# Talking-heads attention and two expert layers on one core: three steps instead of two regrouped inside SBUF, before the rows are stored

## The chip, the cores and the metric

The kernel runs on one core of a Trainium2 chip. The metric is the device time of one execution in microseconds (us). Before the change the median of three runs is 1144.06 us (1140.52 to 1148.41).

## The reference

Four batches of attention with 12 heads, 448 positions and 64 numbers per head; scores are mixed across the heads before the softmax and again behind it. The result goes through two blocks of dense layers. All is float32; the dense matmuls are made of three products of rounded halves.

```python
scores = scale * np.matmul(q, k.transpose(0, 1, 3, 2))
scores = np.einsum('bhij,hg->bgij', scores, w_pre)
attn = softmax(scores)
attn = np.einsum('bhij,hg->bgij', attn, w_post)
x = rows of np.matmul(attn, v)            # 1792 x 768
x = ((x @ w1) * (x @ w2) @ w3) @ w_out
x = np.maximum(np.maximum(x @ m1, x @ m2), x @ m3) @ m_out
```

## The kernel before

**Scores.** A *unit* makes the scores of two heads for 128 queries (a row block): eight matmuls `s<-kall,q` (line 344; the first six units use the three PSUM pairs m, p and s in turn), one eviction with the scale (lines 359 on ACT, 361 on DVE), and a store to DRAM (`sdram`). The six units of batch 0's first row block are evicted into six slices of the large tile `a` (a part of the plan named `arow`); all others go through a ring of two buffers `s`, so the third of them can be evicted only when the store of the first has been read out.

**Regrouping.** The softmax needs the 12 heads of a query beside each other on the partitions. A *step* takes 20 queries: `regroup` brings them into one of three buffers `x`, normally from `sdram` by two copies `x<-sdram`, which wait for the stores of the whole row block. The first steps of batch 0 (those below `FIRST` queries) are copied from `a` inside SBUF, by four copies `x<-a` of five partitions into sixty.

**Step.** The mix `m<-x,kp` (line 407), the maximum `nmax` on DVE (line 411), two exponentials `e` on ACT (line 414), the weights of the second mix (lines 419 to 421), and the second mix `p<-kwr,e` (line 445), whose copy into `a` must wait until the rows in `a` have been copied and stored.

**Dense work beside it.** From the start the kernel also multiplies w3 and w_out together (line 605). Both arrive as 64-bit floats by loads on the POOL queue, 16 tiles of w_out (`early`) and 16 halves of w3 (`wraw`, a ring of three); DVE and ACT turn each into a pair of halves (lines 523 to 528, 535, 537, 570, 571: `hhi`, `hlo` for the first eight tiles of w_out, `yhi`, `ylo` for the others). A load into a used buffer waits until DVE has converted what was in it. Later come the dense layers (line 685) and, behind the planned part, the last two batches (line 221).

**Order.** `Plan` lists every operation with its key (when it is wanted), its inputs and an assumed duration; `order()` runs through them once and writes a fixed order for each engine and for the DMA queue of SP. Engines are in order: an instruction that waits holds all behind it. A DMA that follows eight others on its queues waits until the oldest of these has landed.

Of the kernel before, what the change touches and what calls it, by code (L numbers as in the profile page):

```python
# [18 lines left out]
P = 128  # L19
GI = 10  # L20
# [10 lines left out]
AHEAD = 2  # L31
# [3 lines left out]
HP = H // 2  # L35
# [8 lines left out]
def blocks_of(p):  # L44

    i = 2 * GI * p
    return [[max(0, min(GB, S - i - GI * c - GB * u)) for u in range(2)] for c in range(2)]
# [10 lines left out]
SWITCH = 0.21  # L58
LAND = 2.0
RATE = 0.29  # L60
FIRST = 2 * 2 * GI
BACK = 2.5
STAY = 0.5
QUEUED = 8
# [113 lines left out]
def attention_talking_heads_moe_kernel(  # L178
# [26 lines left out]
    sdram = [dram.tile([S, H, S], F32, name=f"sdram_{b}") for b in range(B)]  # L205
# [59 lines left out]
    def turn(ring, n):  # L265
        used[ring] = used.get(ring, -1) + 1
        return used[ring] % n

    def dma(eng, key, out, src, nbytes, reads=(), writes=()):
        plan(  # L270
            eng, 0.55 if eng == "POOL" else 0.42, key,
            lambda e: ENG[e].dma_start(out() if callable(out) else out, src() if callable(src) else src),
            reads, writes, bytes=nbytes,
        )
# [45 lines left out]
    def load_k(b, pairs, key, eng="SP"):  # L320
        a, z = pairs[0], pairs[-1] + 1
        dma(eng, key, kall[:, a:z], kT[b, :, a:z], 229e3 * (z - a), (), [("k", x) for x in pairs])

    def load_q(b, r, key, eng="SP", after=()):
        w = min(P, S - P * r)
        slot = turn("q", 2)
        dma(eng, key, qs[slot].rearrange("p x j -> p (x j)")[:, :HP * w], qT[b, :, HP * P * r:HP * (P * r + w)],
            3072 * w, list(after), [("q", slot)])
        return slot

    def unit(b, r, u, slot, key, room="s"):

        whole = P * (r + 1) <= S
        parts = [(u, 0), (u, HB)] if whole else [(2 * u, 0), (2 * u + 1, 0)]
        pt = {"m": pm, "p": pp, "s": pz}[room]

        w = min(P, S - P * r)
        q = qs[slot].rearrange("p x j -> p (x j)")[:, :HP * w].rearrange("p (x j) -> p x j", x=HP)

        def multiply(_):  # L340
            for c, (pr, i) in enumerate(parts):
                for o in range(2):
                    sl = slice(o * D, (o + 1) * D)
                    nc.tensor.matmul(  # L344
                        pt[HB * c:HB * c + HB, o, :S], q[sl, pr, i:i + HB], kall[sl, pr], start=True, stop=True
                    )

        bank_of = [(room, x) for x in range(2)]
        plan("PE", 0.76, key, multiply, [("k", pr) for pr, _ in parts] + [("q", slot)], bank_of, mode="q")
        if r == 0 and b == 0:  # L350
            out, where = at.rearrange("p t h i -> p (t h i)")[:, 2 * S * u:2 * S * (u + 1)], ("arow", u)
            out = out.rearrange("p (o j) -> p o j", o=2)
        else:
            n = turn("s", 2)
            out, where = st[n], ("st", n)

        def evict(e):
            if e == "ACT":
                nc.scalar.activation(out, pt[:, :, :S], AF.Copy, scale=D ** -0.5)
            else:  # L360
                nc.vector.tensor_scalar_mul(out, pt[:, :, :S], D ** -0.5)  # L361

        plan({"ACT": 0.95, "DVE": 1.12}, 0, key + 0.05, evict, bank_of, [where])
        if whole:
            x = 0 if r or b else FIRST
            dma("SP", key + 0.06, sdram[b][P * r + x:P * r + P, 2 * u:2 * u + 2], out[x:], 3584 * (P - x), [where],
                [("sd", b, r, u)])
        else:
            for c, (pr, _) in enumerate(parts):
                dma("SP", key + 0.06, sdram[b][P * r:S, 2 * pr:2 * pr + 2], out[HB * c:HB * c + HB], 229e3,  # L370
                    [where], [("sd", b, r, pr)])

    def regroup(b, p, key):
        n = turn("x", AHEAD + 1)
        x = xr[n]
        i = 2 * GI * p
        rows = range(i // P, (min(i + 2 * GI, S) - 1) // P + 1)
        reads = [("sd", b, r, pr) for r in rows for pr in range(HP)]
        if b == 0 and i < FIRST:
            row = at.rearrange("p t h i -> p (t h i)")[:, :H * S]  # L380
            for c in range(2):
                for u in range(2):
                    z = i + GI * c + GB * u
                    dma("SP", key, x[HB * u:HB * u + MR, c], row[z:z + GB], 108e3,
                        [("arow", pr) for pr in range(HP)], [("x", n, u, c)])
        elif i + 2 * GI <= S:
            src = sdram[b][i:i + 2 * GI].rearrange("(c u i) h j -> u (i h) c j", c=2, u=2)
            for u in range(2):
                dma("SP", key, x[HB * u:HB * u + MR], src[u], 215e3, reads, [("x", n, u, 0), ("x", n, u, 1)])
        else:  # L390
            for u, m in enumerate(blocks_of(p)[0]):
                src = sdram[b][i + GB * u:i + GB * u + m].rearrange("i h j -> (i h) j")
                dma("SP", key, x[HB * u:HB * u + m * H, 0], src, 21504 * m, reads, [("x", n, u, 0), ("x", n, u, 1)])
        return n
# [67 lines left out]
    def load_v(b, key, after=()):  # L462
        n = S // P
        dma("SP", key, vt[:, :n], v[b, :P * n].rearrange("(c p) e -> p c e", p=P), 1180e3, (), [("v", 0)] + [("v", 0, x, z) for x in range(n) for z in range(2)])
        dma("SP", key, vt[:S - P * n, n], v[b, P * n:], 197e3, list(after), [("v", 1)])
# [564 lines left out]
    LAST = len(steps)  # L1030
# [14 lines left out]
    def attention_parts():  # L1045

        load_k(0, [0, 1], -20.0, "ACT")
        slot = load_q(0, 0, -20.0)
        load_k(0, [2, 3], -19.9)
        load_k(0, [4, 5], -19.8, "ACT")  # L1050
        block_diagonals(-19.0)
        for u in range(HP):
            unit(0, 0, u, slot, -8.0 + 0.1 * u, "mps"[u % 3])
        todo = [(0, r, u, (0.5 * u, 3 + u, 8.5 + 0.5 * u)[r - 1])
                for r in range(1, 4) for u in range(HP if r < 3 else 3)]
        for b in range(1, B):
            todo += [(b, r, u, NP * b - 11 + 6 * r + u) for r in range(4) for u in range(HP if r < 3 else 3)]
        due = {}
        for b, r, u, s in todo:
            due.setdefault(int(s), []).append((b, r, u))  # L1060
        slots = {}
        xn = {}
        for s in range(AHEAD):
            xn[s] = regroup(*steps[s], -7.0 + 0.1 * s)
        slots[0, 1] = load_q(0, 1, -5.6, after=[("arow", 2)])
        yield -1.0
        en = {}
        for s in range(LAST + LAG):
            if s == 1:
                load_v(0, 3.0, [("arow", 5)])  # L1070
            for d in (s + 2,):
                for b, r, u in due.get(d, []):
                    if u == 0 and (b, r) not in slots:
                        slots[b, r] = load_q(b, r, s)
                    if u == 0 and r == 0 and b:
                        for x in range(0, HP, 2):
                            load_k(b, [x, x + 1], s + 0.1 * x)
            if s + AHEAD < LAST:
                xn[s + AHEAD] = regroup(*steps[s + AHEAD], s - 0.5)
            for x, (b, r, u) in enumerate(due.get(s, [])):  # L1080
                unit(b, r, u, slots[b, r], s + 0.5 * x)
            if s < LAST:
                en[s] = softmax(*steps[s], xn[s], s)
            if s >= LAG:
                b, p = steps[s - LAG]
                post(b, p, en[s - LAG], s)
                if p == NP - 1 or p % CP == CP - 1:
                    attend(b, p, s + 0.97)
                    if p == NP - 1 and b + 1 < B:
                        load_v(b + 1, s + 1.0)  # L1090
            yield s + 0.03
# [16 lines left out]
    def summing():  # L1108
        yield TURN + 0.9
        yield from sum_parts(sums_at)  # L1110

    streams = [attention_parts(), dense_stream(), summing(), second_stream(), tail_stream()]
    heads = [(-20.0 + x, x) for x in range(5)]
    heapq.heapify(heads)
    pool_users = []
    while heads:
        _, x = heapq.heappop(heads)
        n = len(plan.ops)
        key = next(streams[x], None)
# [62 lines left out]
```

## Time and profile before

| | |
|---|---|
| median of three runs | 1144.06 us |
| the profiled execution | 1145.06 us |
| its span, first to last instruction | 1143.3 us |
| outside the span | 1.8 us |
| TensorE (PE) busy | 1102.1 us, 96% of the span |
| DVE, ACT busy | 782.7, 566.2 us |
| mean granted clock | 0.984 of full speed |

Busy time of PE is 96%, but in the first of forty slices it is 3 tenths. Idle time of another engine matters only where PE waits for it. The granted clock is the share of 2.4 GHz that TensorE was given; 0.50 is 1.2 GHz.

### The profile page before, as it was taken

Reading aid. Unit: us, or ns where it says so; the run is one execution under the profiler, and the core shown is the slowest. Engines: PE = TensorE matmul, PEld = TensorE weight load, DVE = VectorE, ACT = ScalarE, POOL = GpSimd, SP = SyncE. Lnnn points to the kernel's source line nnn. Section 1 sums busy time; section 2 is a strip of 40 time slices with the busy share of each in tenths; the row PEclk is TensorE's granted clock in tenths of the full one; section 3 lists DMA queues with packets and bytes.
Section 4 is the critical chain, followed back from the end, with each engine's and each line's share of the span. In section 5 each row is a group of like instructions: output and inputs, shape, how many; then the busy total and the mean of one; then the engine's idle time right before and its main releaser. Section 6 shows DMA issues by size and latency. Waiting matters only on the chain.

```text
span 1143.3 us, 29211 instructions
## 1 busy us (share of the span) xinstructions
PE 1102.1 (96%) x12348; PEld 889.4 (78%) x12348; DVE 782.7 (68%) x1343; ACT 566.2 (50%) x1071; POOL 73.6 (6%) x141
## 2 busy tenths in 40 slices
PE   3999999999999999999999989998999999999998
PEld 1466777787877877777777868887988899888877
DVE  3666785686766777767576676774877764587874
ACT  4576475566654677655445353533433343333331
POOL 3100010000000000000110101100000000000000
PEclk8799999999999999999999999999999999999999
DMA  8798887989874999888899898856433421233343
GB/s 305 217 334 247 282 292 256 311 297 319 303 260 155 311 332 303 291 268 283 284 312 316 271 308 267 283 195 222 148 117 97 120 77 46 76 99 116 107 115 117
DMA packets 106205, 258.95 MB, mean 226 GB/s; under 512 B 20278, under 2 KB 57162, under 8 KB 106074
## 3 DMA queue, kind: packets, MB, share of 16 engines
q1 hardware_dynamic: 88474, 175.79, 47.7%
q0 software_dynamic: 15584, 77.62, 20.5%
q10 hardware_dynamic: 2016, 3.67, 0.9%
q8 instruction: 97, 1.59, 0.6%
q14 instruction: 34, 0.28, 0.1%
HBM read 174.27 MB, written 81.91 MB: 224 GB/s over the span
## 4 chain that ended last, share of the span: by engine, by line
PE 84%; DMA 6%; issue 4%; DVE 3%; ACT 2%; POOL 0%; SPq 0%; DVEq 0%; ACTq 0%; POOLq 0%
PE w L685 28%; PE w L221 8%; PE p L445 7%; PE p L479 6%; PE p L221 6%; PE m L407 6%; PE w L605 6%; PE m L221 6%; PE s L221 5%; PE s L344 5%; DMA x<-a 1%; DMA sdram<-a 1%; DMA wc<-kept_b 1%; DMA vlo<-sums_o 1%; DMA wc<-kept_m 1%
## 5 line engine op out<-in xcount | busy, mean ns | idle before, releaser
L445 PEld LDWEIGHTS p<-kwr,e 60*64 60x64 f32 x5760 | 103.3, 137 | 45.3 <-issue 28.4
L411 DVE TENSOR_REDUCE nmax<-m 128x2 f32<-128x896 f32 (+1 forms) x92 | 100.1, 1088 | 53.7 <-PE m L407 53.2
L414 ACT ACTIVATE e<-m,nmax 128x448 f32<-128x448 f32 (+1 forms) x184 | 115.0, 633 | 36.6 <-DVE nmax L411 36.1
L407 PE MATMUL m<-x,kp 60*64 60x448 f32 x720 | 98.0, 565 | 16.7 <-DMA x<-a 13.0
L445 PE MATMUL p<-kwr,e 60*64 60x60 f32 x5760 | 106.4, 221 | 5.0 <-DVE xlo L489 2.9
L277 ACT COPY a<-p 128x480 f32<-128x480 f32 (+1 forms) x97 | 53.5, 574 | 93.5 <-PE p L445 84.9
L685 PE MATMUL w<-yhi,whi 128*128 128x448 f32 x216 | 83.3, 385 | 0.0
L685 PE MATMUL w<-yhi,wlo 128*128 128x448 f32 x216 | 79.4, 368 | 0.0
L685 PE MATMUL w<-ylo,whi 128*128 128x448 f32 x216 | 79.3, 367 | 0.0
L344 PE MATMUL s<-kall,q 64*64 64x448 f32 x640 | 79.0, 564 | 0.2 <-DVE s L361 0.2
L479 PEld LDWEIGHTS p<-a,v 128*64 128x64 f32 x1536 | 73.7, 137 | 5.9 <-issue 4.8
L479 PE MATMUL p<-a,v 128*64 128x120 f32 (+1 forms) x1536 | 77.6, 260 | 0.0
L685 PE MATMUL w<-xhi,whi 128*128 128x448 f32 x192 | 73.8, 384 | 0.0
L277 DVE COPY a<-p 128x480 f32<-128x480 f32 (+1 forms) x83 | 53.2, 652 | 29.9 <-ACT a L277 23.1
L685 PE MATMUL w<-xhi,wlo 128*128 128x448 f32 x192 | 70.2, 366 | 0.0
L685 PE MATMUL w<-xlo,whi 128*128 128x448 f32 x192 | 70.0, 365 | 0.0
L747 ACT CAST whi<-wlo 128x768 fp32r<-128x768 f32 x39 | 32.6, 835 | 73.6 <-DMA wlo<-sums_m 17.9
L685 PE MATMUL w<-hhi,whi 128*128 128x448 f32 x168 | 64.1, 382 | 2.6 <-ACT whi L660 1.8
L661 DVE TENSOR_TENSOR wlo<-wlo,whi 128x768 fp32r<-128x768 f32 (+1 forms) x52 | 52.8, 1015 | 20.1 <-ACT whi L660 19.8
L407 PEld LDWEIGHTS m<-x,kp 60*64 60x64 f32 x720 | 24.0, 135 | 53.7 <-issue 37.3
L685 PE MATMUL w<-hhi,wlo 128*128 128x448 f32 x168 | 61.5, 366 | 0.8 <-DVE wlo L661 0.8
L221 PE MATMUL p<-t,vhi 128*128 128x448 f32 x204 | 61.7, 372 | 0.5 <-DVE r L934 0.4
(237 smaller groups left out, 2531.3 us busy)
## 6 DMA issues: line engine op xcount, KB each, us to landing
x<-sdram SPq DMA_DIRECT2D x172, 210.0 KB
sdram<-s SPq DMA_DIRECT2D x66, 448.0 KB
wraw<-in_wm POOLq DMA_DIRECT2D x18, 768.0 KB, 7.1
wlo<-kept_m SPq DMA_DIRECT2D x27, 384.0 KB
wlo<-kept_w SPq DMA_DIRECT2D x18, 512.0 KB
wraw<-in_w3T POOLq DMA_DIRECT2D x16, 512.0 KB, 7.2
kept_m<-wc SPq DMA_DIRECT2D x18, 384.0 KB
wc<-kept_m POOLq DMA_DIRECT2D x18, 384.0 KB, 6.0
```

The source lines that it names most:

```text
L221: nc.tensor.matmul(out, w, r, start=(k == 0), stop=(k == 3 * n_k - 1))
L277: (nc.scalar.copy if e == "ACT" else ENG[e].tensor_copy)(out, src)
L344: nc.tensor.matmul(pt[HB * c:HB * c + HB, o, :S], q[sl, pr, i:i + HB], kall[sl, pr], start=True, stop=True)
L407: nc.tensor.matmul(pm[HB * c:HB * c + HB, u, :S], kp[sl], x[sl, c], start=True, stop=True)
L411: plan("DVE", 1.1, key + 0.01, lambda _: nc.vector.tensor_reduce(out=nmax[:r], in_=pm[:r, :, :S], axis=AX.X, op=ALU.max, negate=True), m_b ...
L414: plan("ACT", 0.85, key + 0.02, lambda _, u=u: nc.scalar.activation(e_[:r, u], pm[:r, u, :S], AF.Exp, bias=nmax[:r, u:u + 1], scale=1.0, a ...
L445: nc.tensor.matmul(pt[HB * side:HB * side + HB, c, t, :, u * GB:u * GB + m], e_[sl, u, j:j + HB], kwr[sl, u, :, :m], start=True, stop=True,)
L479: nc.tensor.matmul(pt[o * D:(o + 1) * D, x, pr % 3, :], vt[:, jc, h * D:(h + 1) * D], a[:, jc, h, :], start=(jc == 0), stop=(jc == JC - 1),)
L605: nc.tensor.matmul(pw[b][:, :FW], w, r, start=(k == 0 and i == 0), stop=(k == KH - 1 and i == 2))
L661: plan("DVE", 0.16 + 0.8 * f, key - 0.9, lambda _: nc.vector.tensor_sub(lo, t, hi.bitcast(F32)), h, l)
L685: nc.tensor.matmul(pw[w][:, :S], u, r, start=(k == 0 and i == 0), stop=(k == nk - 1 and i == 2))
L747: nc.scalar.copy(hi, t)
```

## The change

`FIRST` goes from 40 to 60 queries, so that step 2 too is copied from `a`, and the first row block is stored from row 60 on: 68 rows in place of 88. The six stores of these rows are collected in `later` and listed behind the first three regroupings, with a later key (1.5 in place of 0.06 behind the unit's), and each now waits for all six evictions. Step 2 is regrouped at the start; in the loop the next one is step 3.

```diff
-FIRST = 2 * 2 * GI
+FIRST = 3 * 2 * GI
...
+    later = []
+
     def unit(b, r, u, slot, key, room="s"):
...
             x = 0 if r or b else FIRST
-            dma("SP", key + 0.06, sdram[b][P * r + x:P * r + P, 2 * u:2 * u + 2], out[x:], 3584 * (P - x), [where],
-                [("sd", b, r, u)])
+            reads = [where] if r or b else [("arow", y) for y in range(HP)]
+            later.append(lambda: dma(
+                "SP", key + (0.06 if r or b else 1.5), sdram[b][P * r + x:P * r + P, 2 * u:2 * u + 2], out[x:], 3584 * (P - x), reads,
+                [("sd", b, r, u)]))
+            if r or b:
+                later.pop()()
...
-        for s in range(AHEAD):
+        for s in range(AHEAD + 1):
             xn[s] = regroup(*steps[s], -7.0 + 0.1 * s)
+        while later:
+            later.pop(0)()
...
-            if s + AHEAD < LAST:
+            if AHEAD < s + AHEAD < LAST:
                 xn[s + AHEAD] = regroup(*steps[s + AHEAD], s - 0.5)
```

The changed program's lines stand 2 to 8 further down; the operations are named the same. Its orders differ as follows.

SP's queue from its start, before (`q` are queries, `kall` keys, `sdram_75` the score rows of batch 0 in DRAM):

```order
L272 DMA q<-in_qT 128x768
L272 DMA kall<-in_kT 128x896
L272 DMA sdram_75<-a 88x896 x6
L272 DMA x<-a 60x1x448 x8
L272 DMA q<-in_qT 128x768
L272 DMA x<-sdram_75 60x2x448 x2
L272 DMA sdram_75<-s 128x896
L272 DMA x<-sdram_75 60x2x448 x2
```

and of the changed kernel:

```order
L272 DMA q<-in_qT 128x768
L272 DMA kall<-in_kT 128x896
L272 DMA q<-in_qT 128x768
L272 DMA x<-a 60x1x448 x12
L272 DMA sdram_75<-a 68x896 x6
L272 DMA sdram_75<-s 128x896
L272 DMA x<-sdram_75 60x2x448 x2
L272 DMA sdram_75<-s 128x896
L272 DMA q<-in_qT 128x768
L272 DMA sdram_75<-s 128x896
```

The copies inside SBUF stand ahead of the stores now, the second row block's queries are loaded at once, and its first store and the copies of step 3 stand behind the six stores.

PE's start, behind its first five units, of the changed kernel (before, the sixth unit is followed by the first mix at once):

```order
L346 MATMUL s<-kall,q 64x448 x16
L611 MATMUL w<-hhi,whi 128x384
L611 MATMUL w<-hlo,whi 128x384
L611 MATMUL w<-hhi,wlo 128x384
L611 MATMUL w<-hhi,whi 128x384
L611 MATMUL w<-hlo,whi 128x384
L611 MATMUL w<-hhi,wlo 128x384
L413 MATMUL m<-x,kp 64x448 x4
```

Three units of the second row block and the dense work of two tiles of w_out have come ahead of the first mix.

ACT, where the third unit of the second row block is evicted (`s<-s`), and what stands behind it up to the twelfth tile of w_out (the last `yhi`), in the changed kernel:

```order
L576 CAST yhi<-v 128x384 x2
L420 ACTIVATE e,den<-m,nmax 128x448
L277 COPY t<-w 128x384
L361 ACTIVATE s<-s 128x896
L533 ACTIVATE wraw<-wraw 128x512
L531 ACTIVATE wc<-wc 128x512
L533 ACTIVATE early<-early 128x384
L541 CAST whi<-wc 128x512
L531 ACTIVATE v<-v 128x384
L576 CAST yhi<-v 128x384
```

and before:

```order
L570 CAST yhi<-v 128x384
L277 COPY t<-w 128x384
L359 ACTIVATE s<-s 128x896
L570 CAST yhi<-v 128x384
L527 ACTIVATE early<-early 128x384
```

Before, it is the fourth unit of the second row block that is evicted at this place; in the changed kernel it is the third.

## Rows read from the trace of the kernel before

**Rows 1.** Page, 40 slices: busy tenths of PE.
```profile
PE   3999999999999999999999989998999999999998
```
**Rows 2.** Windows: us, PE, PEld, DVE, ACT, POOL busy (instructions), granted clock, DMA share, GB/s.
```profile
0.00:65.00 65.00, 41.35 (x232) 19.80 (x236) 35.99 (x77) 36.66 (x76) 16.58 (x34) 0.77 0.82 273
```
**Rows 3.** Waits, 0 to 60 us: total us, times, longest.
```profile
POOL early L272 <- DVE v L523: 23.3, 4, 10.9
PE m L407 <- DMA x<-a: 13.0, 2, 12.6
ACT e L414 <- DVE nmax L411: 10.2, 1, 10.2
ACT s L359 <- PE s L344: 4.4, 1, 4.4
```
**Rows 4.** Timeline of SP's queue: start, us, what.
```profile
8.24 6.06 SPq L272 DMA_DIRECT2D sdram<-a  x6
14.35 13.63 SPq L272 DMA_DIRECT2D x<-a  x8
```
**Rows 5.** Timeline of PE and ACT: start, us, what, wait ahead of it.
```profile
25.33 1.72 PE L407 MATMUL m<-x,kp 60*64 60x448 f32 x2 [12.58 <-DMA x<-a]
27.51 5.01 PE L407 MATMUL m<-x,kp 60*64 60x448 f32 x6 [0.46 <-DMA x<-a]
62.08 0.90 ACT L359 ACTIVATE s<-s 128x896 f32<-128x896 f32 x1
64.44 1.37 PE L344 MATMUL s<-kall,q 64*64 64x448 f32 x8
```
**Rows 6.** Windows: first the columns of rows 2, then PE alone with its clock, DMA share, GB/s.
```profile
20.00:22.00 2.00, 0.00 (x0) 0.00 (x0) 1.69 (x4) 1.73 (x4) 0.54 (x1) 0.50 0.71 286
...
0.00:14.30 14.30, 7.29 (x48) 1.00 0.88 307
33.50:36.00 2.50, 1.72 (x8) 0.50 0.32 125
```
**Rows 7.** DMA queues, 33.5 to 36 us: packets, MB, share of 16 engines.
```profile
q1 hardware_dynamic: 103, 0.17, 18.0%
q0 software_dynamic: 41, 0.14, 14.2%
```
**Rows 8.** DMA issues, 0 to 60 us: operation, times, KB each (us to landing).
```profile
early<-in_w_out POOLq DMA_DIRECT2D x16, 384.0 KB, 8.5
wraw<-in_w3T POOLq DMA_DIRECT2D x7, 512.0 KB, 7.9
sdram<-a SPq DMA_DIRECT2D x6, 308.0 KB
sdram<-s SPq DMA_DIRECT2D x3, 448.0 KB
...
q<-in_qT SPq DMA_DIRECT2D x3, 384.0 KB
kall<-in_kT ACTq DMA_DIRECT2D x2, 448.0 KB
x<-a SPq DMA_DIRECT2D x8, 105.0 KB
```
**Rows 9.** Timeline of POOL: start, us, what, wait ahead of it.
```profile
50.33 0.53 POOL L272 DMA_DIRECT2D wraw<-in_w3T  x1 [12.81 <-DVE v L523]
50.85 2.66 POOL L272 DMA_DIRECT2D early<-in_w_out  x5
```
**Rows 10.** Chain of waits, 300 to 400 us: start, us, what.
```profile
308.69 0.75 PE m L407 x8
...
311.12 5.06 PE w L685 x24
...
339.79 1.42 PE w L685 x6
341.20 0.91 PE s L344 x8
```

## Prediction

> **What bounds the kernel now.** I read the page's slices first: PE is busy 3 tenths of the first 28.6 us and nearly all of every later slice [rows 1]. The window of the first 65 us has PE busy for 41.35 of them [rows 2]. So a microsecond saved before 65 us should arrive at the end of the kernel, as long as PE's later work stays the same.
>
> The waits name what is late at the start [rows 3]. PE waits 13.0 us for the copies `x<-a`, and behind the first mix everything stands in line: ACT waits 10.2 us for the maximum, DVE sits in front of the same mix, and POOL waits 23.3 us in all for DVE to convert tiles of w_out so that the next may be loaded, and once 12.81 us before a half of w3 [rows 9]. SP's queue tells why the copies are late [rows 4]: six stores are issued from 8.24 us, the eight copies behind them from 14.35. The first mix starts at 25.33 us and drags to 32.5, because its four copies land one after another [rows 5]; the clock is 0.50 all that time [rows 6]. So the start is bound by the DMA queue, then by the conversions on ACT and DVE that the stall held up, not by PE's work.
>
> **Term 1: the copies come first.** They can still not be issued before the last eviction, so from 14.35 us on, as now; but no store lies ahead of them. The four of step 0 are 420 KB. Between 33.5 and 36 us the DMA engines are 0.32 busy with 125 GB/s [rows 6], while both queues have work, SP's with 18.0% and POOL's with 14.2% of the 16 engines [rows 7]. 0.32 of 16 is five: I read this as a copy of five partitions lying on five engines, at 25 GB/s each, and what POOL has loaded sharing them about evenly. Step 0's four copies then take 430 kB / 125 GB/s = 3.4 us alone and 6.9 us shared: they land at about 18 to 22 us in place of 25 to 31.
>
> PE's order now has three more units and the work on two tiles of w_out ahead of the first mix, and the second tile waits for DVE: one eviction and fifteen conversions stand ahead of it from 14 us on, 9 us at the pace of four in 2 us [rows 6], and I add 2 us of waits for ACT, so about 25 us. So the mix should end near 28 us in place of 32.5, bound by conversions and not by the copies; the work ahead of it is work that PE does later now. What counts is ACT, which loses 10.2 us at the first mix and 4.4 us behind the second, at a unit that stands behind that mix [rows 3]: 14.6 us. I take 1 us to remain at each mix, and 3.6 us to come back as waits between DVE and ACT in conversions that have been ready in a heap so far. That leaves 9 us. ACT then comes to the eviction which it does at 62.08 us now [rows 5] at about 53, and POOL's load which waits until 50.33 us [rows 9] is issued near 40.
>
> Step 2's two copies from DRAM become four of 105 KB inside SBUF, the last of twelve. At 6.9 us for every four they have landed by 35 us; its mix is due near 38, so the dense work hides them. The queries' load moves ahead, 384 KB in the first 5 us, hidden behind the first units; if that cover is gone it is 384 KB at 307 GB/s [rows 6], 1.3 us.
>
> **Term 2: the stores come last, and are narrower.** This is the wait I expect in the old one's place. The six stores shrink from 308 KB [rows 8] to 68/88 of that, 238 KB, 1.46 MB in all. The trace shows no store of 68 rows. Those of 88 rows move 286 GB/s at a DMA share of 0.71 [rows 6], 0.71 x 16 = 11 engines of 26 GB/s; the copy of five rows holds five. So one end is 1.46 MB at 286 GB/s, 5.1 us, the other 1.46 MB at 125 GB/s, 11.7 us, both without sharing. In kind the 88-row store is nearest, but both row counts are split evenly, 11 x 8 and 5 x 1, and 68 goes evenly into neither. The largest even split of 68 over at most 16 engines is 4 x 17. I take four engines at 26 GB/s, 14.0 us, and these four among the copies' five: a reading of two rows, and the doubtful point of this forecast.
>
> The Trainium skill (DMA: Bandwidth & Descriptors, section "Why a DMA increments its semaphore by 16 and not by 1") states this as a rule that speaks against the change: the engines of a DMA are the largest number up to 16 that divides the slowest dimension of both sides, and on SP's queue the lowest-numbered ones. The trace agrees with the number at both row counts (0.71 and 0.32 of the engines); which ones they are no row here shows. By that rule the sum would be the one taken here, and with a store as wide as the 88-row one that of the first rival.
>
> Those four engines carry, from 14.35 us on, 12 copies x 105/5 = 252 KB, six stores x 238/4 = 357 KB and then the first store of the ring `s`, 448/16 = 28 KB [rows 8]: 637 KB each, 25.1 us at 26 GB/s, so 39.5 us with nothing else. POOL's loads share them. Left over at 14.35 us: 5.6 MB asked for by then (two loads of queries, three of keys, two halves, six tiles [rows 8]) less 14.3 us x 307 GB/s [rows 6], 1.2 MB, 72 KB an engine; then five tiles and three halves of w3, 5 x 24 + 3 x 32 = 216 KB; near 40 us one half and five tiles, the batch of [rows 9], 152 KB. Together 440 KB, 17 us. The last store of the chain lands between 39.5 and 57 us; since the batch at 40 us comes while the stores still run, I take 56.
>
> Who waits? ACT's eviction of the third unit of the second row block goes into the buffer that this store of the ring reads. It is due at 53 us and gets its buffer at 56: 3 us, ACT standing. Behind it in ACT's order are six conversions, some 0.5 us each by the pace of [rows 6], before the twelfth tile of w_out is ready; before the change that tile came right behind the eviction. So PE has this tile at 56 + 0.9 + 3.1 + 0.5 for DVE, and is through with it at about 61 us in place of 64.4, where the unit starts now [rows 5]. PE has done the same dense work, mixes and second mixes by then, but one unit less, 0.9 us. Gain of the start: 64.4 - 61 - 0.9 = 2.5 us of the 9.
>
> On SP the two copies of step 3 wait for all six stores and hold the two other stores of the ring. Its mix stands behind the twelfth tile, at 61 us or later; the copies go out near 56, so I cost this at nothing, and at up to 3 us if they meet a full queue.
>
> **Term 3: PE changes kind less often.** In the planned part the order goes from dense work to attention and back some 118 times before and 108 now; one of the ten is in the start, and two I leave out as lying beside waits. A block of 6 dense matmuls costs 1.42 us, one of 24 costs 5.06, so 6 without the change of kind 1.21; a block of eight behind dense work costs 0.91, behind its like 0.75 [rows 10]. A round trip is 0.21 + 0.16 = 0.37 us, eight are 3.0 us. The bounds are 0 and 3.7.
>
> **Sum.** 2.5 + 3.0 = 5.5 us. The profiled execution is 1145.06 us (span 1143.3 and 1.8 around it), so 1139.6; it lies 1.0 above the median of the runs, which gives 1138.5.
>
> **Rivals.**
> - *The stores are wide.* On eleven engines they are 130 KB each and not 357, so the chain lands 227 KB, 8.9 us, earlier, at 47: ACT never stands. Then 9 - 0.9 + 3.0 = 11.1 us, 1133. For it: the 88-row store is the same instruction. Against: its 0.71, which points to a split by rows.
> - *The stores hold the start longer than the old copies did.* If POOL's packets take more than half of the four engines, its next loads, three halves of w3 (96 KB, 3.8 us), are served first too and the chain lands at 61 to 63 us. The old pace is reached when it lands at 58.5 (56 + 2.5). At 63 the start is 4.5 us later than now, and the six copies of steps 3 to 5, all behind the stores on SP, add some 2.5 us: with the 3.0 us of term 3 that is 1148. For it: at 36 us [rows 7] the last of the eight copies had still not landed, though issued by 28. Against: POOL's share there was below SP's.
> - *Nothing arrives.* Conversions on ACT and DVE pace the start whoever comes first, and the fewer changes of kind lie beside waits: 1143 to 1145. For it: DVE and ACT are busy 1.69 and 1.73 of 2 us at 20 us, before the mix blocks them [rows 6]. Against: the stall of 10.2 us is no conversion.
>
> **How the numbers follow.** The forecast has a chance of 0.52, wide stores 0.20, nothing arrives 0.16, held longer 0.12. The range is 1131 to 1149: the wide stores with 2 us to spare, and the held start with 1. A measurement of this kernel tells about 1% from no change, 11.4 us. Below 1132.6 lie half of the wide stores and little of the forecast, 0.14; above 1155.5 only a held start that costs twice as much, 0.03; the rest, 0.83, is within.
>
> **What would show it.** Right: the first mix starts before 27 us and runs without gaps; the DMA share stands near 0.25 in some stretch between 30 and 56 us while SP's queue has stores; ACT's longest wait after 40 us is at the eviction into `s`, for a DMA; PE is busy all the time from some 62 us. Wrong in term 2: a DMA share near 0.7 with stores, or ACT not waiting there. Wrong in term 1: the first mix waits for `x<-a` again. Wrong in term 3: the stretch from 100 us to the end is as long as before for the same work. The forecast as a whole is wrong outside its range, or if the gain comes from a stretch beyond 100 us by more than 4 us.

## The result, and the profile after

The changed kernel takes 1153.64 us (median of nine runs, 1150.51 to 1158.04), the kernel before 1142.21 beside it. The ratio is 1.0096, with a 95% interval of 1.0073 to 1.0118: some 11 us slower, where 5.5 us faster were forecast. The profiled execution takes 1153.67 us, 1151.9 of them its span.

What the start has lost is seen at one place that both kernels pass: the first product with `v`. PE's timeline (start, us, what), first of the kernel before:

```profile
95.37 5.14 PE L479 MATMUL p<-a,v 128*64 128x120 f32 x96
```

and after:

```profile
104.07 5.14 PE L485 MATMUL p<-a,v 128*64 128x120 f32 x96
```

From there to the end of the span it is 1143.3 - 95.37 = 1047.9 us before and 1151.9 - 104.07 = 1047.8 after. So the difference of the two traces, 8.7 us, lies in the first 104 us. (The medians differ by 11.4: the execution traced before the change is 2.9 us above its median of nine.) The window of the first 65 us after (columns of [rows 2]):

```profile
0.00:65.00 65.00, 34.06 (x220) 19.31 (x220) 32.66 (x72) 32.61 (x67) 16.08 (x33) 0.78 0.70 244
```

PE was busy for 41.35 of the 65 us before [rows 2] and is for 34.06 now. Where it stands, its timeline shows; the answer to [rows 5]:

```profile
25.39 1.36 PE L413 MATMUL m<-x,kp 60*64 60x448 f32 x8
...
34.67 0.96 PE L413 MATMUL m<-x,kp 60*64 60x448 f32 x2 [1.97 <-DMA x<-a]
...
37.53 1.75 PE L413 MATMUL m<-x,kp 60*64 60x448 f32 x2 [1.89 <-DMA x<-a]
...
54.09 0.34 PE L611 MATMUL w<-yhi,wlo 128*128 128x384 f32 x1
68.29 1.77 PE L346 MATMUL s<-kall,q 64*64 64x448 f32 x8 [13.87 <-ACT s L361]
```

The first mix runs without a gap, done before 27 us. At 54 us PE has all behind it that it had at 64.44 before [rows 5] but one unit. Then it stands for 14 us. ACT's timeline names the cause:

```profile
52.38 0.48 ACT L277 COPY t<-w 128x384 f32<-128x384 f32 x1 [0.29 <-PE w L611]
67.32 0.92 ACT L361 ACTIVATE s<-s 128x896 f32<-128x896 f32 x1 [14.46 <-DMA sdram<-s]
```

ACT is at the eviction of the third unit at 53 us and gets its buffer at 67.3. SP's timeline shows what was queued ahead of the store that it waits for (answer to [rows 4]):

```profile
13.35 16.12 SPq L272 DMA_DIRECT2D x<-a  x12
29.52 14.27 SPq L272 DMA_DIRECT2D sdram<-a  x6
43.89 4.65 SPq L272 DMA_DIRECT2D sdram<-s  x1
66.29 0.80 SPq L272 DMA_DIRECT2D x<-sdram  x2
```

The chain of waits has this store in it for as long as that:

```profile
43.89 23.41 DMA sdram<-s
```

Issued at 43.89, landed at 67.3, behind the six stores of 68 rows. They have landed themselves by 66.29, when SP is free to issue `x<-sdram`. The windows (us, PE busy, clock, DMA share, GB/s) show how they moved:

```profile
57.00:59.00 2.00, 0.00 (x0) 0.50 0.29 118
59.00:61.00 2.00, 0.00 (x0) 0.50 0.25 104
61.00:63.00 2.00, 0.00 (x0) 0.50 0.26 106
```

Nothing runs on PE (nor on DVE or ACT from 55 to 66 us), and the DMA engines are 0.25 busy: four of sixteen, 26 GB/s each.

The trace also keeps the updates of each DMA's semaphore. Apart from one that comes within half a us of the end of the issue, a store of 68 rows has four, a copy of five partitions five, and the ring's store sixteen; I read each as one engine whose part has landed. Of the ring's store twelve come from 51.3 to 52.6 us and the last four from 64.3 to 67.3: only the parts on the four engines of the narrow stores were held. SP's queue from 50 to 52 us (packets, MB, share of the 16 engines) has more than those four at work:

```profile
q1 hardware_dynamic: 122, 0.40, 49.5%
```

### The profile page after: what moved, and what is told of

Read it like the earlier page. It is cut to its first block, busy times and chain, and to the rows that moved or that the text cites. A ratio compares the mean times of both kernels' runs of the same rounds, so it can differ in the third digit from the quotient of the medians.

```text
span 1151.9 us, 29191 instructions
## 1 busy us (share of the span) xinstructions
PE 1098.0 (95%) x12348; PEld 891.9 (77%) x12348; DVE 787.2 (68%) x1351; ACT 562.5 (49%) x1063; POOL 73.8 (6%) x141
## 4 chain that ended last, share of the span: by engine, by line
PE 87%; DMA 6%; DVE 4%; ACT 2%; SPq 1%; issue 1%; DVEq 0%; ACTq 0%
PE w L691 31%; PE w L221 8%; PE p L451 7%; PE p L485 7%; PE p L221 6%; PE m L413 6%; PE w L611 6%; PE m L221 6%; PE s L346 5%; PE s L221 5%; DMA sdram<-s 2%; DMA x<-a 1%; SPq L272 1%; DMA vlo<-sums_o 1%; DMA wc<-kept_m 1%
## 5 line engine op out<-in xcount | busy, mean ns | idle before, releaser
L451 PE MATMUL p<-kwr,e 60*64 60x60 f32 x5760 | 103.9, 219 | 6.4 <-DVE xlo L495 3.1
L346 PE MATMUL s<-kall,q 64*64 64x448 f32 x640 | 80.7, 575 | 22.4 <-ACT s L361 16.7
L413 PE MATMUL m<-x,kp 60*64 60x448 f32 x720 | 92.9, 561 | 3.9 <-DMA x<-a 3.9
L277 DVE COPY a<-p 128x480 f32<-128x480 f32 x84 | 53.7, 651 | 29.2 <-ACT a L277 16.4
L534 DVE SCALAR_TENSOR_TENSOR wc<-wc,wraw 128x768 uint32<-128x768 uint32 (+1 forms) x56 | 48.9, 877 | 28.5 <-ACT wc L531 28.3
```

The lines of the kernel that those rows point to most:

```text
L277: (nc.scalar.copy if e == "ACT" else ENG[e].tensor_copy)(out, src)
L346: nc.tensor.matmul(pt[HB * c:HB * c + HB, o, :S], q[sl, pr, i:i + HB], kall[sl, pr], start=True, stop=True)
L413: nc.tensor.matmul(pm[HB * c:HB * c + HB, u, :S], kp[sl], x[sl, c], start=True, stop=True)
L451: nc.tensor.matmul(pt[HB * side:HB * side + HB, c, t, :, u * GB:u * GB + m], e_[sl, u, j:j + HB], kwr[sl, u, :, :m], start=True, stop=True,)
L534: plan("DVE", 0.16 + 0.8 * f, key, lambda _: nc.vector.scalar_tensor_tensor(ti, ti, 3, word(0), op0=ALU.logical_shift_left, op1=ALU.bitwis ...
```

## The experiments

Twelve kernels. In six of them only the rows of the six stores differ from another kernel, and PE, ACT, DVE and POOL have its order word for word: with 80, 72 and 69 rows that of the changed kernel, with 92 and 96 that of the kernel before, and the last that of the fifth. Rows that a store takes beyond the needed ones are read by nobody; no kernel leaves anything out of the computation. Each ratio is against the kernel before.

**Stores of 80 rows.** Sixteen engines could share them evenly, five rows each.

```diff
-sdram[b][P * r + x:P * r + P, ...], out[x:]
+sdram[b][P * r + min(x, P - 80):P * r + P, ...], out[min(x, P - 80):]
```

> The changed kernel, its orders unchanged, but the six late stores take 80 rows (48 to 127) in place of 68. Narrow-store theory (68 rows lie on four DMA engines, and the first store of the ring s waits behind them on those four): 80 rows go evenly over 16 engines, 105 KB each and not 357, so the ring's store lands at least 10 us earlier, ACT's wait of 14.5 us at its eviction is under 3 us, PE's wait of 13.9 us is gone, and the time is 1132 to 1140 us, below the kernel before. Rival (the place of the stores, behind twelve copies on SP and followed by everything else, costs the time however wide they are): 18% more bytes in the same place, ACT still waits 12 us or more, 1150 to 1158 us.

Measured: 1143.92 us (1140.55 to 1147.21), ratio 0.9999 (0.9981 to 1.0017). The loss is gone, by storing more. But no gain appears, and the time lies between the two ranges, so the first theory holds for the width and misses the rest. ACT's timeline has the eviction on time, and another one late:

```profile
54.29 0.92 ACT L361 ACTIVATE s<-s 128x896 f32<-128x896 f32 x1 [1.14 <-DMA sdram<-s]
63.74 0.92 ACT L361 ACTIVATE s<-s 128x896 f32<-128x896 f32 x1 [4.35 <-DMA sdram<-s]
```

and PE's the mix of the fourth step between them:

```profile
59.52 3.66 PE L413 MATMUL m<-x,kp 60*64 60x448 f32 x8 [3.28 <-DMA x<-sdram]
```

What stands behind the late stores on SP, the fourth step's rows and the second store of the ring, is late although the stores are wide.

**Stores of 69 rows**, the other way (69 = 3 x 23), the same line with 69 in place of 80.

> The changed kernel, its orders unchanged, but the late stores take 69 rows in place of 68. Narrow-store theory: 69 splits evenly over three engines only (3 x 23), each gets 483 KB and not 357, 5 us more alone and up to 10 us shared; the DMA share falls to about 0.19 while they are alone, ACT waits 19 to 25 us, 1158 to 1164 us. Rival (the place, or the bytes): 1.5% more bytes, within 1 us of the changed kernel, 1152 to 1155 us.

Measured: 1160.01 us (1158.35 to 1160.87), ratio 1.0137 (1.0107 to 1.0167). One row more costs another 0.0041 in the ratio, some 5 us, as expected; ACT's wait, 17.71 us, is a little below the 19 to 25 forecast. The window in which only the stores run:

```profile
63.00:65.00 2.00, 0.00 (x0) 0.50 0.19 79
```

0.19 of 16 is three engines, again 26 GB/s each.

**92 rows in the kernel before** (92 = 4 x 23), where 88 are needed.

```diff
-sdram[b][P * r + x:P * r + P, ...], out[x:]
+sdram[b][P * r + min(x, P - 92):P * r + P, ...], out[min(x, P - 92):]
```

> The kernel before, its orders unchanged (stores ahead of the copies), but the early stores take 92 rows in place of 88. Narrow-store theory: 92 splits evenly over four engines (4 x 23) and not over eleven, 483 KB each and not 168, the copies behind them on these engines land 13 to 25 us later, so the first mix starts at 38 to 50 us in place of 25 and the time is 1153 to 1168 us. Rival (bytes and order alone count): 4.5% more bytes, the first mix within 1 us of 25, 1141 to 1144 us.

Measured: 1155.63 us (1152.62 to 1158.98), ratio 1.0102 (1.0067 to 1.0136). The width alone, without the change, costs as much as the change. PE's first mix:

```profile
42.02 5.48 PE L407 MATMUL m<-x,kp 60*64 60x448 f32 x8 [29.05 <-DMA x<-a]
```

It starts 16.7 us later than in [rows 5].

**96 rows in the kernel before** (96 = 16 x 6), the same line with 96.

> The kernel before, its orders unchanged, but the early stores take 96 rows in place of 88. Narrow-store theory: 96 goes over all 16 engines, 126 KB each and not 168, the first mix starts 1.5 to 3.5 us earlier, 1138 to 1141 us. Rival (bytes count): 9% more bytes, 0.5 us later, 1142 to 1144 us.

Measured: 1144.77 us (1137.04 to 1147.62), ratio 0.9999 (0.9977 to 1.0022). The profiled first mix starts at 23.18 us in place of 25.33, as the first theory has it, but its gain doesn't arrive: eleven engines against sixteen make no difference in the time.

**Three steps inside SBUF, stores ahead of the copies, 80 rows.** The third step is kept, the order undone (`order()` then lists the engines' work anew, as for the changed kernel).

```diff
-later.append(lambda: dma("SP", key + (0.06 if r or b else 1.5), ...
+dma("SP", key + 0.06, sdram[b][P * r + x:P * r + P, ...], out[x:], ..., [where], ...   # x = 48
```

> Three steps are regrouped inside SBUF, but the stores stay ahead of the copies, as in the kernel before, and take 80 rows each (16 engines; the twelve rows 48 to 59 among them nobody reads). Theory 'late stores' (what costs in the changed kernel is only that the narrow stores stand late on SP, ahead of the ring's first store): SP is past the stores at 13 us and past the twelve copies near 34 (12 x 1.7 us), the first mix starts near 23 as in the kernel before with 96 rows, the first store of the ring lands before 40 and no eviction waits for it; first attend 91 to 95 us, time 1136 to 1143. Rival 'five-engine copies' (a third step regrouped inside SBUF is slow in itself, four more copies of five partitions ahead of everything else on SP): the second and third mix wait for x<-a past 38 and 45, first attend at 98 or later, time 1146 to 1152.

Measured: 1135.97 us (1134.07 to 1138.33), ratio 0.9943 (0.9921 to 0.9964): the first to beat the kernel before, and the fastest of all. SP's timeline and PE's:

```profile
8.22 6.28 SPq L272 DMA_DIRECT2D sdram<-a  x6
14.56 14.98 SPq L272 DMA_DIRECT2D x<-a  x12
```

```profile
21.80 5.22 PE L409 MATMUL m<-x,kp 60*64 60x448 f32 x8 [8.86 <-DVE hlo L573]
...
90.40 5.14 PE L481 MATMUL p<-a,v 128*64 128x120 f32 x96
```

The second mix waits for `x<-a` twice, 1.82 and 2.69 us, until 40.59, as the rival said; but the third, at 46.94, doesn't wait, and the first product with `v` comes 5.0 us earlier than before. The details of the first theory failed in one place: the ring's first two stores leave only at 51 us, not before 40, since PE's order has its units later. ACT waits only 1.9 us for the ring's stores up to 85 us, in two waits. From 50 to 65 us PE is busy for 11.15 us before and 13.30 here:

```profile
50.00:65.00 15.00, 11.15 (x54) 0.90 1.00 327
...
50.00:65.00 15.00, 13.30 (x83) 1.00 1.01 377
```

**The stores between the copies of the second and the third step, 80 rows.**

```diff
-"SP", key + (0.06 if r or b else 1.5), sdram[b][...
+"SP", key + 0.06 if r or b else -6.85 + 0.001 * u, sdram[b][...
```

> The changed kernel with stores of 80 rows that stand between the copies of the second and of the third step, not behind all twelve. Theory 'late stores': the first store of the ring still stands behind all of them and lands near 52, so only the rows that the fourth step reads arrive earlier (x<-sdram near 47 in place of 52): the 3.3 us that the fourth mix waited with 80 rows behind all copies go, the third mix waits for its own copies instead, time 1139 to 1146, level with the kernel before. Rival 'five-engine copies': the stores of 16 engines pass between the copies in 5 us, everything behind is unchanged in number, time as with 80 rows behind all copies, 1140 to 1147; the two are told apart by the fourth mix's wait and by the span, not by the time alone.

Measured: 1139.46 us (1135.93 to 1143.11), ratio 0.9967 (0.9951 to 0.9983). As the first theory has it, the fourth mix no longer waits (it runs at 60.98) and the third waits for its copies (1.1 us, at 51.45). It is a little faster than before, not level.

**Four steps inside SBUF, 48 rows, behind the first twelve copies.**

```diff
-FIRST = 3 * 2 * GI
+FIRST = 4 * 2 * GI
```

> Four steps regrouped inside SBUF: stores of 48 rows (48 = 16 x 3, 16 engines), behind the first twelve copies, and four more copies behind them. Theory 'late stores': the six stores move 1.03 MB, 3 to 4 us on 16 engines, the first store of the ring lands near 45, before ACT's eviction at 53, and PE doesn't stop for it; the fourth mix takes its rows from the copies near 50; first attend 90 to 95, time 1134 to 1142. Rival 'five-engine copies': sixteen copies take 25 us or more of SP, the fourth mix waits until 55 or later, time 1143 to 1150.

Measured: 1142.19 us (1135.68 to 1149.77), ratio 0.9994 (0.9972 to 1.0016), between the two ranges. The first store of the ring has landed by 49.1 us, and ACT doesn't stop for it. But the fourth mix runs only at 63.17, not near 50: its four copies, issued from 45.64 on, land from 52.8 to 63.6. That part is the rival's. (The trace is of the slowest of the twelve runs, 1149.77.) SP's timeline shows the stores ahead of them:

```profile
30.72 13.37 SPq L272 DMA_DIRECT2D sdram<-a  x6
```

48 rows on sixteen engines take SP 13.4 us to issue, about as long as 68 rows on four (14.27). From the second on, each is issued when the copy eight places ahead of it has landed (the third at 38.40, that copy at 38.38): behind twelve copies the queue moves at the pace of what is ahead on it.

**The order alone: two steps inside SBUF, 88 rows, behind the eight copies.**

```diff
-FIRST = 3 * 2 * GI
+FIRST = 2 * 2 * GI
-for s in range(AHEAD + 1):
+for s in range(AHEAD):
-if AHEAD < s + AHEAD < LAST:
+if s + AHEAD < LAST:
```

> The order alone: two steps inside SBUF as before, stores of 88 rows (11 engines) behind the eight copies. Theory 'late stores': SP is past the copies near 27, the stores (1.9 MB at 286 GB/s, 6.6 us) land near 36, the third step's rows near 41 and the first store of the ring near 40, all ahead of their need at 47 and 53; the first mix comes near 26 with no wait for x<-a behind it, and the 9 us that the early copies bring stay in part: first attend 88 to 94, time 1134 to 1141, faster than before. Rival 'stores last never pays' (each store behind the copies comes as late as the copies came early): the third mix waits for x<-sdram until 48 or later, time 1142 to 1150.

Measured: 1144.51 us (1141.31 to 1146.93), ratio 1.0011 (0.9994 to 1.0029). The rival was right: the first mix starts at 25.59 us and runs freely, and the third waits for what the stores held up:

```profile
51.70 0.96 PE L413 MATMUL m<-x,kp 60*64 60x448 f32 x2 [1.48 <-DMA x<-sdram]
53.88 1.77 PE L413 MATMUL m<-x,kp 60*64 60x448 f32 x6 [1.23 <-DMA x<-sdram]
```

**The changed kernel, the ring's first two stores on ACT's queue.**

```diff
-"SP", key + ...
+"ACT" if (b, r) == (0, 1) and u < 2 else "SP", key + ...
```

> The changed kernel with its six stores of 68 rows late on SP as they are; only the first two stores of the ring s leave on ACT's DMA queue in place of SP's. Theory 'held on the queue' (the ring's store lands late because it stands behind the narrow stores on one queue, and 12 of the 16 engines could serve it at once): on a queue of its own it is issued at 43 to 46 and lands near 50, ACT's eviction at 53 doesn't wait for it, PE goes on where it stood for 14 us; the rows of the fourth step still wait for the narrow stores, past 60, so the time is 1143 to 1149. Rival 'held on the engines' (the four engines serve what came first, whichever queue it is on; a transfer is done when its last engine is): the store lands at 62 or later as before, and the time is 1150 to 1156.

Measured: 1154.7 us (1152.19 to 1155.94), ratio 1.0114 (1.0081 to 1.0146). Both expectations failed in part. ACT issues the store only at 53.17 us, in its own order, and it has landed by 61.2; its eviction, which stands behind more conversions in this kernel's order, waits less than 1 us:

```profile
53.17 0.33 ACTq L272 DMA_DIRECT2D sdram<-s  x1
...
61.18 0.92 ACT L361 ACTIVATE s<-s 128x896 f32<-128x896 f32 x1 [0.91 <-DMA sdram<-s]
```

So 8 us on a queue of its own in place of 23.4, though issued 9 us later. Its last four engines landed at 61.0 to 61.2, while SP's narrow stores went on landing on their four until 71.05: it was held on SP's queue, not by the engines. But the time doesn't fall. The narrow stores themselves end later (SP issues `x<-sdram` at 71.19, not 66.29). PE now stands at the next thing that needs them, the rows of the fourth step:

```profile
74.15 2.65 PE L413 MATMUL m<-x,kp 60*64 60x448 f32 x8 [17.96 <-DMA x<-sdram]
```

The ring's store was only the first of two waits; both hang on the narrow stores.

**Four steps inside SBUF, the stores of 48 rows first.**

```diff
-FIRST = 3 * 2 * GI
+FIRST = 4 * 2 * GI
-later.append(lambda: dma("SP", key + (0.06 if r or b else 1.5), ...
+dma("SP", key + 0.06, ..., [where], ...
```

> A version meant to beat both kernels: four steps regrouped inside SBUF, the stores ahead of the copies and of 48 rows each (16 engines, 1.03 MB in place of the 1.72 MB with 80 rows ahead of the copies). Theory 'late stores': the stores pass in 3 to 5 us, the first mix starts at 20 to 23, the copies end near 40, and no eviction waits for a store of the ring: time 1132 to 1139, level with the 1136 of three steps and 80 rows or better. Rival 'five-engine copies': the copies of the fourth step take 5 us of SP just where the ring's stores begin, as in the version with the 48-row stores behind the copies; the ring's stores come late and the time is 1139 to 1146.

Measured: 1138.41 us (1135.27 to 1142.07), ratio 0.997 (0.9951 to 0.9989): in the first range, yet not better than three steps. The details failed from the first mix on: it starts at 28.64 us, not at 20 to 23. The load of the second row block's queries stands behind five stores now, and PE waits for it, ahead of that mix:

```profile
21.23 1.77 PE L346 MATMUL s<-kall,q 64*64 64x448 f32 x8 [9.45 <-DMA q<-in_qT]
```

And the chain of waits has a store of the ring in it, issued right behind the last four copies:

```profile
36.46 26.21 DMA sdram<-s
```

That is the rival's place. Its semaphore tells why it took until 62.7 us: eleven engines have landed their parts by 44.6, the other five at 50.1 to 62.7. Five is the number of engines of a copy, and the last copy ahead of it lands at 60.3. POOL's loads have 56% to 79% of the 16 engines in the stretches of 6 us from 36 to 60 us. ACT waits 3.06 us for this store.

**Stores of 72 rows in the changed kernel** (72 = 12 x 6).

```diff
-sdram[b][P * r + x:P * r + P, ...], out[x:]
+sdram[b][P * r + min(x, P - 72):P * r + P, ...], out[min(x, P - 72):]
```

> The changed kernel with stores of 72 rows (48 + 8 more than needed: 56 to 127), the order as it is. Theory 'as many engines as the largest number up to 16 that divides the rows': 72 lies on 12 engines, 0.75 of them, and with 1.55 MB it behaves as the 80 rows did: the first store of the ring lands near 54, time 1140 to 1148, some 10 us below the changed kernel for four rows more per store. Rival 'only a multiple of 16 is fast' (other row counts fall far back): the store lands past 62 and the time is 1149 to 1156.

Measured: 1142.86 us (1137.77 to 1151.07), ratio 1.0008 (0.9984 to 1.0032). Four rows more in each store take the loss away; a multiple of 16 is not needed. ACT's eviction, at its time:

```profile
52.54 0.92 ACT L361 ACTIVATE s<-s 128x896 f32<-128x896 f32 x1 [0.27 <-DMA sdram<-s]
```

The Trainium skill (DMA: Bandwidth & Descriptors, section "Why a DMA increments its semaphore by 16 and not by 1") has the engines as the largest number up to 16 that divides the slowest dimension of both sides. With the rows as this dimension it would be 4 for 68, 3 for 69, 12 for 72. The traces agree: the semaphores count 4, 3 and 12 late updates, and the shares were 0.25 and 0.19.

**The version with stores of 80 rows first, with 68 rows.**

```diff
-x = 0 if r or b else P - 80
+x = 0 if r or b else FIRST
```

> Three steps inside SBUF, the stores ahead of the copies, and of 68 rows: the version with 80 rows ahead of the copies (1136) with nothing but the row count changed; PE's, ACT's and DVE's order is the same. Theory 'four engines, whatever the order': the narrow stores hold SP and four of the five engines that the copies use, as with 92 rows in the kernel before: the first mix starts at 36 to 43 us in place of 22, first attend at 101 to 107, time 1147 to 1155. Rival 'only late narrow stores hurt' (ahead of the copies they land before POOL's loads come in, and nobody needs their rows early): first mix before 30, time 1135 to 1143.

Measured: 1144.39 us (1142.17 to 1146.01), ratio 1.0018 (1.0004 to 1.0033). In its trace the first theory is right, in size it is off by 2.6 us (1147 was its lower end) and by 1.1 at the first product with `v`. The window in which the stores are under way, and the first mix:

```profile
18.00:20.00 2.00, 0.00 (x0) 0.50 0.28 114
```

```profile
36.79 5.52 PE L409 MATMUL m<-x,kp 60*64 60x448 f32 x8 [24.18 <-DMA x<-a]
...
99.86 5.14 PE L481 MATMUL p<-a,v 128*64 128x120 f32 x96
```

The first mix comes 15 us later than with 80 rows, the first product with `v` 9.5.

**What the twelve say together.** With three steps inside SBUF:

| | stores ahead of the copies | stores behind them |
|---|---|---|
| 80 rows | 0.9943 (1135.97 us) | 0.9999 (1143.92 us) |
| 68 rows | 1.0018 (1144.39 us) | 1.0096 (1153.64 us) |

Each ratio has an interval of about 0.002 to either side. In all the traces the semaphores count the engines of a store: 4 for 68 and 92 rows, 3 for 69, 11 for 88, 12 for 72, 16 for 48, 80 and 96.

The change is three edits in one. The third step inside SBUF, with the orders that follow from it, gains 0.57%, some 6.5 us. (Its stores have 80 rows for 88; that this counts for nothing I take from the 96 rows in the kernel before, it wasn't run by itself.) The order takes that back: 0.0056 in the ratio with 80 rows, 0.0078 with 68. The narrower store adds 0.0097 behind the copies and 0.0075 ahead of them. With two steps inside SBUF the order costs nothing that can be told (1.0011 against the kernel before).

## Why the prediction was wrong

**Term 1, the copies come first: right for the first mix, too early for the later copies.** The first mix starts at 25.39 us for a forecast of 25 and is done before 28; ACT is at the eviction at 53 us, as forecast; POOL's half of w3 is issued at 42.24 for "near 40". What it missed is that the copies of steps 1 and 2 land late: the second mix waits twice for `x<-a`, 1.97 and 1.89 us, and ACT still waits 6.43 us for a maximum at 40.44. The eighth copy lands at 37.5 us, and the last, the twelfth, at 43.3, not by 35.

**Term 2, the stores come last and are narrower: right in kind, wrong in size, and this is the step that failed.** Four engines at 26 GB/s was right (0.25, 104 GB/s), and so were the instruction that waits and the store it waits for. Forecast was a landing at 56 us and a wait of 3; it landed at 67.3, past the upper bound of 57, and ACT waited 14.46.

The sum went wrong in what it asked of the four engines: 637 KB of SP's own and 440 KB of POOL's at 26 GB/s. Its upper bound counted all of POOL's loads ahead of the ring's store, so their order alone can't have passed it. Two stretches make up the 11 us, an estimate that takes POOL's bytes as spread evenly over the 16 engines.

The first ends at 43.3 us, with the twelfth copy. The queues from 14.35 to 43.3 us after (packets, MB, share of the 16 engines):

```profile
q0 software_dynamic: 1076, 4.69, 47.7%
q1 hardware_dynamic: 847, 1.52, 16.2%
```

That is 293 kB of POOL's and 258 kB of copies on each of the engines that the copies use, 551 kB in 28.95 us: 19 GB/s, where the forecast had 26 and 21 us. Some 8 us are lost here. The forecast's pace came from one stretch of 2.5 us in which POOL had little to load [rows 7]. Why the engines are slower while copies and loads share them, no run settles. From 25 to 34 us:

```profile
q0 software_dynamic: 657, 2.72, 87.9%
q1 hardware_dynamic: 132, 0.22, 9.2%
```

The five engines of the copies are 31%; SP's queue has 9% of the 16, less than a third of its five, where term 1 took an even split.

In the second stretch, from 43.3 to 66.2 us, six stores (365 kB on each of the four) and 3.54 MB of POOL's (221 kB) pass at 25.6 GB/s, as forecast. But the batch that POOL issues from 42 us on is larger: to 52 us three halves of w3 and five tiles, 3 x 32 + 5 x 24 = 216 KB an engine, where the forecast counted 152. That is another 2.5 us, and the two are some 10 of the 11.

The rival "held longer" named two parts of this: POOL ahead on the narrow engines, and its next halves served first. It put the landing at 61 to 63 and the break-even at 58.5. At the true landing its rule gives 67.3 - 58.5 = 8.8 us of loss, and the first product with `v` is 8.7 us late; so close an agreement is partly luck, for the rule went by the twelfth tile, which was not what PE waited for. The rival was given 0.12, and its price of 1148 took off 3.0 us for term 3 that did not come.

The effect on PE was told wrongly in that detail: it was to need the twelfth tile of w_out next, and needs the unit whose bank the late eviction empties. And the fourth step's rows, costed at nothing to 3 us, were a second wait of at least the same length: with the ring's store on another queue PE waited 17.96 us for them. Taking away the one wait that the forecast had seen gains nothing. A third buffer for the ring, which would take away the same wait, wasn't tried.

**Term 3, fewer changes of kind on PE: not seen.** 3.0 us were to come off the planned part, and "as long as before" from 100 us on was to show it wrong. It is as long: 1047.9 us before, 1047.8 after. Up to the last product with `v` of the planned part the changed kernel is 4.0 us quicker (784.56 - 104.07 = 680.5 against 779.91 - 95.37 = 684.5), and behind it 3.9 us slower. But the 4.0 are not the order's: with 92 rows, where PE's order is that of the kernel before, the same stretch takes 787.42 - 106.50 = 680.9. Behind the planned part the loss recurs: the four traces of the changed order with stores behind the copies (68, 69, 72 and 80 rows) take 365.6 to 367.3 us there, the three of the order before (88, 92 and 96) 363.4 to 364.3. What costs these 1 to 4 us no run looked for. From the first product with `v` to the end the same order takes 1045.9 to 1047.8 us in three traces (68, 72 and 80 rows, behind the copies), and before's 1044.9 to 1047.9 in three. A gain of 3 us over the whole can't be seen in these traces, and the medians show no sign of one: the loss at the start alone, 8.7 us, is most of the ratio.

**The cases.** "Wide stores" at 1133 was priced by what the copies gain, without what is lost behind late stores: with stores of 80 rows behind the copies the time is 1143.92, no gain at all. "Nothing arrives", 1143 to 1145, gave that time, but for another reason: conversions on ACT and DVE.

## What to carry to other kernels

The number of engines of a DMA followed from its row count at every count tried here: before changing a row count, divide it. 68 rows cost 10 us against 72 or 80, and padding a transfer with rows that nobody reads was cheaper than the right number of them. When a step moves behind others on one queue, list every reader of what then stands behind it, not only the first; here two long waits stood there, and removing one showed nothing. An edit made of several parts deserves one run for each: the useful part of this one, a third step inside SBUF, gains 0.57% when the stores stay ahead and are 80 rows wide.

## What was not expected of the hardware

A narrow transfer holds what stands behind it on the same queue, on its own engines, although that uses all sixteen: behind the stores of 68 rows the ring's store was done on twelve engines at 52.6 us and on the last four at 67.3; on ACT's queue, issued 9 us later, it was done on all by 61.2, with the narrow stores still on their four.

Between the queues the sharing was not always even. Of the engines that its narrow transfers lie on, SP's queue had 29% from 25 to 34 us (9.2 of 31) and half from 58 to 62:

```profile
q1 hardware_dynamic: 64, 0.22, 13.4%
q0 software_dynamic: 57, 0.20, 12.3%
```

In the first of these stretches SP's packets were 1.7 KB on average and POOL's 4.1, in the second 3.4 and 3.5. Taking turns by packet would give SP 29% and 50%. From 46 to 48 us (3.2 and 4.6 KB) it would give 41%, and the trace has 49 (12.3 of 25); so this is a reading, which no run tests.

And behind the stall the granted clock is 0.50, 1.2 GHz, until 77 us (PE had stood from 54 to 68), and the first matmuls of a dense product take 0.52 us in place of 0.33:

```profile
75.47 0.52 PE L611 MATMUL w<-ylo,whi 128*128 128x384 f32 x1
```
